# All queries and keys transposed by TensorE instead of the DMA crossbar in a gated linear attention with a feed-forward layer

## The chip, the core and the metric

The kernel runs on one core of a Trainium2 chip. The metric is the device time in microseconds of one execution. It is 247.29 us, the median of three runs of the kernel before (247.19 to 247.33).

## The reference

The inputs are q, k, v and the complex decay a_re + i a_im, each 4 batches x 8 heads x 768 steps x 48 channels in f32, and three weights of a gated layer (384 x 1536, 384 x 1536 and 1536 x 384). The reference is a recurrence over time per batch and head, and then the gated layer over its 3,072 rows:

```
mag = sqrt(a_re^2 + a_im^2);  scale = min(mag, 0.999) / (mag + 1e-6)
for t in range(768):
    S_re, S_im = ar*S_re - ai*S_im + k[t] (x) v[t],  ar*S_im + ai*S_re
    y[t] = q[t] . S_re                       # 48-vector times 48x48 state
x   = y, heads side by side, [3072, 384]
out = (sigmoid(x @ w_gate) * (x @ w_val)) @ w_out
```

## The kernel before

Time is cut into 6 chunks of 128 steps. One batch of one chunk is a slab, so there are 24 slabs m = 0 to 23, each with all 8 heads. Slabs are handled in groups of 2 or 4 (`SIZES`, line 51) in the stage on decays, and in pairs (`PAIR`) in the feed-forward layer.

For each slab the kernel loads a_re, a_im, k, q and v (SP queue, line 552), takes logarithms and angles of the decays, sums them over the chunk with a triangular matmul (steps `cl` and `ct`), and turns the sums into scale and phase (`ee`, `cs`). Step `qke` (line 728) scales q and k, and step `qs` (line 851, always on VectorE) multiplies them by cosine and sine into an f16 tile `slot`, in which each head has 128 columns: time in the 128 partitions.

The scores of a head need k and q with channels in the partitions, so `slot` is transposed: 8 blocks of 128x128 for q and 8 for k per slab. The code has two ways to do it, chosen by `m in CROSSED` (line 866):

- `tp` and `qkT` (lines 888 to 902): for each half of a slab, 8 TensorE transposes against an identity into one PSUM bank (lines 892 and 893), then one copy of 128x1024 f16 from PSUM to the tile `qkT`, on VectorE or ScalarE (`copied`, lines 519 and 521), as `HOME["qkT"]` has it.
- `xk` and `xq` (lines 870 to 876): two DMAs per slab with the crossbar's transpose, issued from the SP queue (line 871), which write the two `qkT` tiles from `slot` with no compute engine and no PSUM bank.

In the kernel before, slabs 0 to 5 go the first way and slabs 6 to 23 the second.

From there both ways are alike: `sc` (line 911, 4 matmuls for each half of a slab) makes the scores, `mst` (line 926, VectorE) masks them out of PSUM, `kv` and `P` (lines 958 and 968) add to the state, `u` and `x16` scale it by the chunk's decay, `y` (lines 984 and 986) makes the output rows, `y16`, `xp`, `xt` bring them to f16 and transpose them for the next layer. For each pair of slabs the layer follows: `pg` and `pv` (line 1043, six matmuls of 256 columns each per step), a tanh (line 1054, ScalarE), the product `p` (line 1061, VectorE), `po` (line 1082, 12 matmuls of 384 columns per slab, in three steps), `ot` (out of PSUM) and `st`, the store.

The order of all instructions is written out ahead: each step has a due time in `TIMES`, the steps are emitted sorted by it (`Plan.order`, line 341), and every engine and the SP queue work through their own share of that order without overtaking. The due times are used here only as an order. `SLOTS` says which buffer each tile takes, in the same order. `HOME` says for each step that can run on several engines which one takes it (v VectorE, a ScalarE, g GpSimd). `WARM` (line 303) says ahead of which steps dummy matmuls of 128 columns on zeros are run (line 1131), 131 in all.

Of the kernel before, what the change touches and what calls it, by code (L numbers as in the profile page):

```python
# [27 lines left out]
CROSSED = range(6, 24)  # L28
# [6 lines left out]
    "sq": "vagvaaggaagagagaaggagggg",  # L35
    "add": "vvvvgggggggggggggggggggg",
    "lh": "gvggggvggggg",
    "r": "vvgggggggggg",
    "v16": "vavagaggggagggggagavaaga",
    "qke": "vvvggggvggggggggggggvggg",  # L40
    "th": "aagvaagvgaav",
    "ab": "vvavvavaavaaaaaaaaaavaaa",
    "qkT": "vavavvvvavvvvvvvvvvvvvvvvvvvvvvvvvvvvvvvvvvvvvvv",
    "P": "vava",
    "u": "ggggggvggggggggggvgg",
    "x16": "ggaavgaggggvggag",
    "y16": "avvvaavvavavvvavaaavaaaa",
    "xt": "vvvvvvavvvvvavvavvvvvaav",
    "ot": "vvvvvaaavvvvavvaaavvaaavv",
# [4 lines left out]
        27.89, 36.02, 27.27],  # L54
    "wv": [
        31.35, 38.17, 36.03],
    "wo": [
        53.47, 54.3, 65.03],
    "lr": [
        0.75, 2.68, 7.03, 7.06, 24.34, 27.88, 25.83, 26.32, 45.89, 58.15,  # L60
        53.31, 52.18, 71.46, 92.9, 87.25, 85.33, 106.38, 121.07, 118.57,
        112.93, 170.37, 176.96, 133.38, 160.02],
    "la": [
        2.22, 1.85, 10.78, 7.07, 24.5, 26.36, 25.84, 27.87, 48.76, 56.39,
        53.93, 53.32, 75.86, 92.85, 87.77, 85.34, 111.4, 121.08, 121.86,
        118.56, 176.57, 178.21, 153.22, 134.91],
    "sq": [
        7.04, 7.02, 11.86, 9.9, 24.95, 29.54, 26.34, 29.5, 49.21, 58.89,
        56.85, 62.71, 83.72, 96.51, 92.96, 86.01, 112.9, 129.56, 128.24,
        118.61, 180.83, 185.55, 167.29, 170.36],  # L70
    "add": [
        7.05, 7.9, 13.4, 13.88, 26.35, 38.15, 28.5, 38.12, 53.3, 65, 62,
        65.86, 87.2, 96.54, 96.47, 92.92, 121.81, 129.58, 128.25, 129.55,
        184.23, 185.57, 169.56, 170.39],
    "lna": [
        9.92, 14.99, 33.31, 67.86, 98.47, 139.01, 185.56, 171.42],
    "lh": [
        8.54, 14.47, 40.53, 42.65, 69.29, 75.89, 102.61, 103.34, 136.22,
        141.84, 185.59, 172.91],
    "lnm": [  # L80
        11.87, 15.39, 38.16, 66.46, 100.65, 132.15, 185.58, 170.4],
    "inv": [
        9.93, 16.37, 36.01, 70.07, 103.36, 139.02, 186.18, 172.85],
    "r": [
        10.77, 19.16, 40.52, 39.65, 73.59, 75.88, 108.19, 107.9, 142.65,
        142.64, 189.11, 173.82],
    "cl": [
        14.97, 14.96, 17.84, 16.27, 45.44, 42.85, 47.17, 46.54, 70.89, 76.95,
        80.11, 77.54, 104.14, 104.52, 114.2, 116.75, 138.97, 140.17, 148.32,
        149.93, 187.16, 186.78, 181.01, 173.23],  # L90
    "ee": [
        16.91, 14.98, 18.49, 17.83, 47.18, 44.65, 48.42, 47.56, 72.96, 79.27,
        86.25, 79.29, 106.53, 106.39, 114.78, 117.62, 140.01, 141.81, 149.19,
        152.85, 189.76, 189.77, 182.5, 173.81],
    "scr": [
        35.3, 38.13, 41.19, 37.26, 52.64, 53.49, 54.34, 53.48, 87.94, 92.86,
        95.76, 92.91, 118.58, 111.43, 121.83, 124.54, 153.21, 155.22, 160.22,
        160.21, 195.89, 195.1, 187.57, 187.58],
    "rbt": [
        46.92, 48.74, 55.48, 96.46, 126.03, 161.47, 198.36, 188.29],  # L100
    "arr": [
        50.09, 50.04, 55.92, 98.24, 127.86, 161.92, 205.03, 188.88],
    "lk": [
        16.93, 15.41, 15.42, 17.85, 30.76, 49.23, 53.94, 66.48, 75.91, 85.35,
        94.86, 88.08, 112.25, 92.84, 112.27, 118.55, 125.19, 156.21, 161.95,
        146.39, 185.54, 190.51, 161.93, 181.02],
    "lq": [
        16.94, 16.28, 16.95, 21.91, 41.18, 50.73, 62.72, 69.68, 79.24, 92.87,
        95.78, 88.09, 112.26, 104.92, 122.21, 118.59, 155.19, 156.9, 161.96,
        146.4, 190.31, 197.73, 161.94, 190.12],  # L110
    "lv": [
        15.4, 29.55, 9.91, 26.79, 30.86, 50.74, 71.28, 66.47, 52.19, 92.94,
        76.96, 95.79, 133.17, 121.82, 125.2, 146.64, 160.01, 154.52, 171.41,
        166.24, 140.93, 180.62, 192.37, 195.11],
    "v16": [
        15.89, 30.3, 14.95, 27.29, 45.52, 60.69, 71.29, 84.58, 87.19, 101.96,
        114.07, 118.91, 136.26, 130.58, 142.92, 147.37, 164.44, 155.21,
        178.63, 169.53, 167.28, 202.72, 198.62, 205.05],
    "qke": [
        17.82, 16.36, 20.04, 24.35, 48.73, 53.28, 67.87, 71.45, 84.59, 93.48,  # L120
        96.49, 92.93, 112.96, 108.55, 134.93, 121.8, 157.53, 160.03, 167.43,
        157.52, 209.72, 205.09, 191.58, 190.32],
    "atan": [
        14.48, 21.92, 40.57, 75.9, 108.2, 143.28, 191.6, 176.95],
    "ct": [
        15.44, 15.43, 22.66, 24.05, 48.2, 49.65, 58.14, 59.2, 83.81, 87.93,
        91.11, 87.21, 116.85, 121.09, 130.19, 122.59, 151.79, 158.27, 164.99,
        155.16, 205.89, 202.2, 191.28, 189.92],
    "r16": [
        15.45, 18.69, 23.57, 25.71, 49.24, 50.7, 58.9, 59.78, 84.57, 89.07,  # L130
        91.94, 87.95, 117.61, 121.2, 132.12, 123.7, 152.84, 159.36, 165.57,
        156.87, 207.37, 204.03, 192.35, 190.49],
    "nid": [
        16.92, 19.28, 24.33, 26.3, 49.49, 52.17, 59.3, 60.37, 85.16, 89.47,
        92.89, 88.87, 118.54, 121.4, 132.33, 124.35, 153.03, 160, 166.46,
        157.5, 208.97, 205.07, 192.97, 191.11],
    "cr": [
        20.92, 23.58, 25.85, 28.76, 50.72, 53.37, 62.74, 64.56, 87.18, 91,
        95.81, 89.85, 119.29, 122.19, 134.27, 126.29, 156.88, 161.48, 167.96,
        157.86],  # L140
    "ab": [
        17.28, 20.91, 26.31, 26.78, 52.62, 53.29, 60.7, 63.2, 87.24, 91.46,
        95.8, 89.46, 118.9, 122.61, 134.26, 126.3, 155.17, 162.17, 167.97,
        158.26, 209.12, 205.47, 195.76, 192.33],
    "cs": [
        21, 23.59, 26.51, 30.73, 52.63, 54.33, 65.04, 65.87, 88.07, 92.06,
        98.25, 91.47, 121.01, 124.52, 134.92, 126.94, 156.89, 162.18, 170.33,
        160.19, 209.71, 205.48, 195.77, 192.34],
    "qs": [
        21.9, 24.04, 29.56, 33.52, 54.31, 56.84, 67.89, 72.97, 89.48, 94.21,  # L150
        98.26, 92.95, 122.6, 125.18, 136.25, 128.26, 157.55, 163.7, 175.58,
        160.2, 210.61, 207.38, 198.38, 192.88],
    "tp": [
        24.94, 24.49, 26.86, 25.82, 30.88, 33.51, 34.4, 34.25, 56.38, 61.19,
        63.19, 59.9],
    "qkT": [
        26.18, 26.33, 27.86, 28.51, 34.86, 34.87, 38.11, 38.14, 59.65, 61.99,
        63.91, 61.2],
    "sc": [
        30.87, 26.8, 29.51, 30.31, 36, 35.29, 39.63, 38.75, 63.38, 62.7,  # L160
        64.55, 65.43, 76.51, 76.73, 80.49, 79.88, 99.76, 98.23, 103.88,
        103.37, 108.76, 108.54, 110.29, 105.52, 133.14, 130.57, 133.37,
        132.11, 144.9, 144.91, 141.57, 146.38, 167.92, 166.23, 170.32, 170.09,
        182.04, 182.27, 179.73, 179.08, 219.4, 218.3, 218.53, 215.46, 205.46,
        204.01, 202.19, 202.47],
    "mst": [
        30.89, 27.26, 31.34, 30.74, 37.25, 35.55, 40.05, 39.66, 64.58, 63.18,
        64.99, 65.85, 79.26, 77.55, 82.04, 82.03, 102, 99.99, 104.53, 103.57,
        110.54, 110.53, 114.09, 106.37, 133.57, 132.13, 134.9, 133.19, 145.74,
        145.73, 144.93, 148.33, 168.49, 167.42, 171.45, 170.52, 184.25,  # L170
        183.56, 182.51, 181.03, 220.93, 221.67, 220.95, 217.02, 205.91,
        204.43, 204.02, 204.04],
    "kv": [
        30.75, 40.06, 77.33, 35.62, 84.19, 72.09, 98.02, 90.24, 111.38,
        111.17, 121.02, 125.17, 144.87, 141.37, 152.83, 166.03, 180.81,
        171.19, 180.6, 186.17],
    "P": [
        39.64, 45.46, 79.28, 40.54, 87.17, 75.87, 101.65, 90.99, 112.95,
        112.94, 121.1, 127.85, 144.94, 142.63, 153.44, 168.15, 183.57, 186.38,
        181.05, 192.36],  # L180
    "y": [
        31.46, 33.3, 37.89, 42.66, 67.91, 67.88, 87.23, 85.97, 102.59, 105.07,
        116.74, 121.03, 136.85, 137.26, 146.6, 148.7, 171.4, 171.84, 186.37,
        183.14, 221.99, 221.25, 207.36, 205.1],
    "y16": [
        34.24, 34.88, 38.76, 42.68, 69.67, 69.27, 88.11, 86.71, 103.55,
        105.77, 116.76, 121.13, 138.98, 139, 148.73, 149.96, 172.01, 172.45,
        187.59, 187.81, 222.6, 222.41, 207.97, 205.88],
    "xp": [
        34.85, 35.83, 41.17, 44.62, 71.27, 70.08, 88.7, 87.76, 104.91, 106.36,  # L190
        121.11, 121.19, 140, 140.55, 149.2, 150.97, 172.9, 173.07, 189.75,
# [970 lines left out]
```

## Time and profile before

| | value |
|---|---|
| median of three runs | 247.29 us |
| profiled execution, its own time | 246.99 us |
| span of that execution, first to last instruction | 244.9 us |
| PE (TensorE) busy | 215.4 us, 88% |
| VectorE (DVE) busy | 206.3 us, 84% |
| ScalarE (ACT) busy | 198.6 us, 81% |
| GpSimd (POOL) busy | 145.9 us, 60% |
| bytes moved by DMA | 41.75 MB, 170 GB/s over the span |
| crossbar DMAs, all on the SP queue | 36, first issued at 72.8 us, last at 218.8 us |
| TensorE's granted clock | 1.000 |

The span is 2.1 us shorter than the execution's own time, since it begins with the first instruction and ends with the last. Busy time of PE includes the pipeline's latency (a matmul of 128 columns is recorded with 219 ns while the next begins 56 ns later), so a busy PE can still have gaps; the starts of the matmuls show these.

### The profile page before, as it was taken

To read this page: it belongs to the slowest core of one execution; us is meant where nothing else is said; L and a number is where in the kernel's file an instruction comes from. 1 tells how busy PE (TensorE), PEld (TensorE's weight loads), DVE (VectorE), ACT (ScalarE), POOL (GpSimd) and SP (SyncE) were. 2 spreads that over 40 slices of the span, in tenths; PEclk is the share of its full clock that TensorE was granted. 3 is DMA by queue.
4 is the path that set the end of the run, shared out by engine and by line. 5 is a ranking of instruction groups with operands and counts; after the bars stand their busy time and mean duration, and the time that the engine had idled before them with its cause. 6 is when DMAs were issued, how large, how long until landed. Compare 5 with 4: busy or idle time off the path is not lost.

```text
span 244.9 us, 6068 instructions
## 1 busy us (share of the span) xinstructions
PE 215.4 (88%) x2319; PEld 168.5 (69%) x2319; DVE 206.3 (84%) x317; ACT 198.6 (81%) x326; POOL 145.9 (60%) x138
## 2 busy tenths in 40 slices
PE   0376899959787997999999999999999999999993
PEld 0234688738556865778867778877788777788981
DVE  4589999999888999999999979989887977988250
ACT  2899899948599989999989999996899995542341
POOL 2305977895567899758659986499776683100000
PEclk9999999999999999999999999999999999999999
DMA  7999999999999999999999998979999569073011
GB/s 144 215 218 212 197 183 192 177 191 175 177 180 137 202 244 186 196 177 219 197 192 205 195 212 172 220 165 178 196 191 205 131 136 197 35 141 98 3 64 66
DMA packets 171004, 41.75 MB, mean 170 GB/s; under 512 B 163916, under 2 KB 170976, under 8 KB 170976
## 3 DMA queue, kind: packets, MB, share of 16 engines
q1 hardware_dynamic: 166800, 37.80, 78.3%
q0 software_dynamic: 4176, 3.57, 9.6%
q8 instruction: 18, 0.29, 0.5%
q14 instruction: 10, 0.08, 0.1%
HBM read 30.67 MB, written 4.72 MB: 145 GB/s over the span
## 4 chain that ended last, share of the span: by engine, by line
PE 50%; DVE 15%; ACT 13%; SPq 8%; DMA 8%; issue 4%; DVEq 0%; ACTq 0%
PE banks L1043 25%; PE banks L1082 15%; SPq L552 7%; DMA qk<-in_q_dram 5%; DVE a L768 3%; DVE slot L851 3%; PE banks L911 2%; DVE p L1061 2%; ACT g L1054 2%; DMA qk<-in_k_dram 2%; PE banks L783 2%; DMA a<-in_a_im_dram 1%; DVE qk L728 1%; DVE r L798 1%; ACT lm L604 1%
## 5 line engine op out<-in xcount | busy, mean ns | idle before, releaser
L1061 DVE SCALAR_TENSOR_TENSOR p<-g,banks 128x512 f16<-128x512 f16 x72 | 47.7, 681 | 12.5 <-ACT g L1054 7.4
L1043 PE MATMUL banks<-xt,wg 128*128 128x256 f16 x432 | 56.0, 273 | 0.7 <-DVE xt L521 0.4
L1043 PE MATMUL banks<-xt,wv 128*128 128x256 f16 x432 | 56.2, 273 | 0.0
L1082 PE MATMUL banks<-wo,p 128*128 128x384 f16 (+1 forms) x300 | 55.5, 320 | 0.5 <-ACT g L1054 0.3
L1054 ACT ACTIVATE g<-banks 128x512 f16<-128x512 f32 x72 | 41.2, 601 | 16.8 <-PE banks L1043 11.6
L1043 PEld LDWEIGHTS <-wg 128*128 128x128 f16 x432 | 40.9, 98 | 7.8 <-issue 1.5
L1043 PEld LDWEIGHTS <-wv 128*128 128x128 f16 x432 | 41.4, 98 | 6.8 <-issue 0.5
L728 POOL TENSOR_TENSOR qk<-qk,ee 128x768 f32<-128x768 f32 x19 | 35.3, 1863 | 14.5 <-ACT cr L815 6.8
L851 DVE TENSOR_TENSOR slot<-qk,banks 128x1536 f16<-128x1536 f32 x24 | 41.8, 1745 | 1.7 <-issue 1.3
L1082 PEld LDWEIGHTS <-p 128*128 128x128 f16 x300 | 27.7, 97 | 14.6 <-issue 1.6
L1125 ACT ACT_TABLE_LOAD x28 | 35.9, 1283 | 0.5
L926 DVE TENSOR_TENSOR mst<-banks,msk_t 128x512 f16<-128x512 f32 x48 | 31.9, 685 | 3.4 <-PE banks L911 2.9
L647 POOL TENSOR_TENSOR a<-a 128x768 f32<-128x768 f32 x10 | 18.7, 1884 | 10.7 <-ACT a L641 8.6
L591 POOL TENSOR_TENSOR lm<-sq 128x384 f32<-128x384 f32 x20 | 21.2, 1064 | 4.2 <-ACT sq L583 3.8
L585 POOL TENSOR_TENSOR sq<-a 128x768 f32<-128x768 f32 x12 | 18.2, 1513 | 6.2 <-DMA a<-in_a_im_dram 4.3
L911 PEld LDWEIGHTS <-qkT 128*128 128x128 f16 x192 | 13.2, 97 | 3.2 <-DVE qkT L521 1.1
L940 POOL TENSOR_TENSOR state<-state,arr 128x384 f32<-128x384 f32 x15 | 12.5, 837 | 4.2 <-DVE arr L697 3.4
L583 ACT ACTIVATE sq<-a 128x768 f32<-128x768 f32 x10 | 8.6, 856 | 7.9 <-DMA a<-in_a_re_dram 7.8
L658 PE MATMUL banks<-lm,wl_t 128*128 128x384 f32 x8 | 4.6, 700 | 10.9 <-ACT lm L604 10.9
L768 DVE SCALAR_TENSOR_TENSOR a<-a 128x768 f16<-128x768 f32 x10 | 13.8, 1409 | 0.0
L798 DVE TENSOR_SCALAR r<-banks 128x384 f16<-128x384 f32 x24 | 13.2, 549 | 0.6 <-PE banks L783 0.4
L815 ACT ACTIVATE cr<-banks 32x384 f32<-32x384 f32 x20 | 9.7, 484 | 4.7 <-PE banks L805 4.0
(93 smaller groups left out, 411.8 us busy)
## 6 DMA issues: line engine op xcount, KB each, us to landing
a<-in_a_re_dram SPq DMA_DIRECT2D x24, 192.0 KB
a<-in_a_im_dram SPq DMA_DIRECT2D x24, 192.0 KB
v<-in_v_dram SPq DMA_DIRECT2D x24, 192.0 KB
qk<-in_k_dram SPq DMA_DIRECT2D x24, 192.0 KB
qk<-in_q_dram SPq DMA_DIRECT2D x24, 192.0 KB
out_dram<-ot SPq DMA_DIRECT2D x23, 192.0 KB
wg<-in_moe_w_gate_dram POOLq DMA_DIRECT2D x3, 384.0 KB, 7.7
wv<-in_moe_w_val_dram POOLq DMA_DIRECT2D x3, 384.0 KB, 10.6
```

The source lines that it names most:

```text
L585: on.tensor_tensor(out=T[SQ], in0=T[A][:, :, s], in1=T[A][:, :, s], op=ALU.mult)
L591: home("add", m).tensor_tensor(out=T[LM][:, s], in0=T[SQ][:, 0], in1=T[SQ][:, 1], op=ALU.add)
L647: home("r", w).tensor_tensor(out=T[A][:, 1, i:j], in0=T[A][:, 1, i:j], in1=T[A][:, 0, i:j], op=ALU.mult)
L728: home("qke", m).tensor_tensor(out=T[QK], in0=T[QK], in1=T[EE], op=ALU.mult)
L768: nc.vector.scalar_tensor_tensor(out=turns(T)[:, i:j, 1], in0=T[A][:, 1, i:j], scalar=1.0 / TWO_PI, op0=ALU.mult, in1=turns(T)[:, i:j, 0], ...
L851: nc.vector.tensor_tensor(out=T[SL].rearrange("p i h (r x) -> p r i h x", r=2)[:, :, :, :, 0:D], in0=T[QK].rearrange("p i (h d) -> p i h d ...
L926: nc.vector.tensor_tensor(out=T[MS][:, :n_], in0=T[SC], in1=msk_t.unsqueeze(1).broadcast_to([L, n_, L]), op=ALU.mult)
L1043: nc.tensor.matmul(T[ACC][:, r], wt[:, j, f0:f0 + 128], T[XT][:, :, j], start=(j == 0), stop=(j == 2))
L1054: nc.scalar.activation(out=T[G16], in_=T[PG], func=FT.Tanh, scale=0.5)
L1061: nc.vector.scalar_tensor_tensor(out=T[PT][:, 2 * fp:2 * fp + 2], in0=T[G16], scalar=1.0, op0=ALU.add, in1=T[PV], op1=ALU.mult)
L1082: nc.tensor.matmul(T[PO][:, :wd], T[PT][:, fb, s0:s0 + L], wo16[:, fb, c0:c0 + wd], start=(fb == 0), stop=(fb == NFB - 1))
L1125: nc.scalar.preload_act_table_set(SETS[key[1]])
```

## The change

The set of slabs that go through the crossbar becomes empty: slabs 6 to 23 are transposed as slabs 0 to 5 were. The 36 steps `xk` and `xq` are gone, 36 steps `tp` (288 TensorE transposes) and 36 steps `qkT` (36 copies out of PSUM) come in. All due times, buffer numbers, engine choices and dummy matmuls are new; the functions of the kernel are as they were. In the diff, each row of `TIMES` and `SLOTS` is replaced; the rows shown are those of the steps that come, go or are referred to.

```
-CROSSED = range(6, 24)
+CROSSED = ()
...
 HOME = {
-    "sq": "vagvaaggaagagagaaggagggg",
+    "sq": "vagvggaagaaagagaggagvggg",
     "add": "vvvvgggggggggggggggggggg",
-    "lh": "gvggggvggggg",
-    "r": "vvgggggggggg",
-    "v16": "vavagaggggagggggagavaaga",
-    "qke": "vvvggggvggggggggggggvggg",
-    "th": "aagvaagvgaav",
-    "ab": "vvavvavaavaaaaaaaaaavaaa",
-    "qkT": "vavavvvvavvvvvvvvvvvvvvvvvvvvvvvvvvvvvvvvvvvvvvv",
-    "P": "vava",
-    "u": "ggggggvggggggggggvgg",
-    "x16": "ggaavgaggggvggag",
-    "y16": "avvvaavvavavvvavaaavaaaa",
-    "xt": "vvvvvvavvvvvavvavvvvvaav",
-    "ot": "vvvvvaaavvvvavvaaavvaaavv",
+    "lh": "vgggggggggvg",
+    "r": "vvggggggvvvg",
+    "v16": "ggggaggaggaaggaggggggaga",
+    "qke": "vvvgvggvgggggggggggggggg",
+    "th": "aavgggagagvg",
+    "ab": "vvvavaavaaaaaaaavaaaaaaa",
+    "qkT": "vvvvvvvvvvvvvvaavvavvvavavvvvvavaaavvvvavaavavva",
+    "P": "vaaa",
+    "u": "ggggggggggggggggvggg",
+    "x16": "gggggaggggaggagv",
+    "y16": "aaavavaaavvaaaavvaavaava",
+    "xt": "vvvvvavvvavvvvavvvvvvaav",
+    "ot": "vvvavavavaavvvvaaaavvavvv",
 }
...
     "tp": [
-        24.94, 24.49, 26.86, 25.82, 30.88, 33.51, 34.4, 34.25, 56.38, 61.19,
-        63.19, 59.9],
+        21.72, 26.53, 26.54, 24.19, 35.45, 34.69, 32.72, 31.38, 60.78, 58.8,
+        60.33, 63.19, 69.1, 64.68, 75.72, 76.17, 92.98, 93.43, 93.88, 98.44,
+        104.97, 105.83, 106.27, 100.4, 125.58, 126.68, 134.63, 128.16, 145.52,
+        144.9, 135.08, 137.45, 168.34, 167.24, 170.05, 174.68, 182.14, 181.14,
+        176.64, 177.73, 220.12, 220.57, 222.63, 223.43, 206.66, 205.57,
+        208.47, 207.36],
...
     "pg": [
-        37.24, 38.1, 43.23, 42.69, 42.7, 36.58, 45.88, 53.92, 55.73, 52.61,
-        49.22, 53.27, 72.29, 79.23, 80.71, 72.95, 74.1, 78.57, 91.95, 89.59,
...
+        38.3, 36.48, 41.11, 37.14, 42.53, 43.58, 51.62, 58.87, 47.73, 47.27,
+        58.82, 54.97, 72.03, 87.31, 79.63, 73.34, 74.86, 72.69, 86.5, 86.49,
...
-    "xk": [
-        75.93, 79.44, 96.52, 102.6, 108.18, 99.11, 126.31, 126.39, 141.85,
-        140.02, 164.45, 167.94, 178.22, 175.93, 215.7, 213.52, 203.36, 202.18],
-    "xq": [
-        75.92, 79.43, 96.53, 102.62, 107.24, 105.51, 126.04, 127.84, 144.86,
-        140.57, 164.49, 167.95, 180.61, 165, 217.04, 214.81, 203.37, 202.14],
 }
...
 WARM = {
-    ('cl', 3): 5,
-    ('ct', 2): 43,
-    ('sc', 0, 1): 3,
-    ('sc', 1, 0): 3,
-    ('sc', 1, 1): 3,
-    ('sc', 0, 0): 11,
-    ('y', 1): 29,
-    ('kv', 3): 4,
-    ('kv', 1): 3,
-    ('pv', 0, 0): 5,
-    ('pv', 1, 4): 3,
-    ('pg', 1, 3): 5,
-    ('ct', 7): 3,
-    ('y', 5): 1,
+    ('cl', 0): 22,
+    ('ct', 1): 5,
+    ('ct', 3): 57,
+    ('sc', 0, 0): 1,
+    ('sc', 1, 1): 4,
+    ('sc', 0, 1): 7,
+    ('y', 1): 34,
+    ('kv', 1): 10,
+    ('kv', 0): 7,
+    ('sc', 3, 1): 4,
+    ('pg', 0, 0): 1,
+    ('pg', 1, 5): 9,
+    ('ct', 7): 10,
+    ('pv', 2, 5): 5,
     ('cl', 8): 5,
-    ('pv', 2, 5): 5,
 }
```

## The prediction

> **What bounds the kernel now.** I read the page's busy times and slices first, to see which engine is full and where.
>
> ```profile
> PE 215.4 (88%) x2319; PEld 168.5 (69%) x2319; DVE 206.3 (84%) x317; ACT 198.6 (81%) x326; POOL 145.9 (60%) x138
> ...
> PE   0376899959787997999999999999999999999993
> ...
> DMA  7999999999999999999999998979999569073011
> ```
>
> Three engines are above 80%, and DMA is at nine tenths for three quarters of the span. PE is full only from the second third on. So the second view is busy time by stretches, cut where the order of steps can be cut too: at 77.6 us the first `pg` of the pair of slabs 4 and 5 starts, at 148.4 us that of slabs 12 and 13.
>
> ```profile
> 0.00:50.00 50.00, 33.38 (x378) 25.87 (x379) 42.50 (x68) 43.17 (x66) 28.26 (x33) 1.00 1.05 193
> 50.00:77.60 27.60, 21.54 (x230) 15.98 (x230) 23.83 (x35) 20.63 (x34) 18.54 (x18) 1.00 1.07 173
> 77.60:148.40 70.80, 67.97 (x741) 52.52 (x740) 66.90 (x103) 67.88 (x109) 57.79 (x51) 1.00 1.04 199
> 148.40:241.00 92.60, 92.54 (x974) 74.17 (x972) 73.03 (x114) 66.44 (x120) 41.31 (x39) 1.00 0.65 139
> ```
>
> After the two times the columns are PE, PEld, DVE, ACT, POOL, granted clock, DMA share, GB/s. From 148.4 us on PE is busy 92.54 of 92.6 us; between 77.6 and 148.4 us all three engines are above 94%. Busy PE can hide gaps, so I took the starts of all matmuls from the timeline and counted as standstill what lies between two starts beyond the pitch of their kind (56 ns for 128 columns, 109 for 256, 162 for 384, 25 for 48): 19.1 us before 77.6, 6.1 us from there to 148.4, 1.0 us after.
>
> Third, the chain in order of time, in the middle and at the end:
>
> ```profile
> 80.42 1.33 SPq L871
> 82.41 3.52 DMA a<-in_a_im_dram
> ...
> 115.54 4.25 DMA qk<-in_k_dram
> ```
>
> ```profile
> 229.18 7.86 PE banks L1043 x72
> 237.04 3.91 PE banks L1082 x24
> 240.97 0.49 ACT ot L512
> ```
>
> Until about 127 us the chain passes through ScalarE, VectorE, the SP queue and loads; from there to 241 us nearly every long piece is PE. In the first part the crossbar does cost: its packets and the loads share engines and the SP queue, which does this in one stretch:
>
> ```profile
> 95.67 0.44 SPq L552 DMA_DIRECT2D qk<-in_q_dram  x1
> 96.16 0.57 SPq L552 DMA_DIRECT2D v<-in_v_dram  x1
> 96.83 8.32 SPq L871 DMA_TRANSPOSE qkT<-slot  x5
> ```
>
> **The change part by part.** What each operation costs is in the rows of slabs 0 to 5, which go TensorE's way already:
>
> ```profile
> L892 PE MATMUL banks<-idn_t,slot 128*128 128x128 f16 x48 | 6.3, 219 | 1.3 <-ACT qkT L519 0.9 <-DVE p L1061 0.3 <-ACT banks L827 0.2
> ...
> L521 DVE COPY qkT<-banks 128x1024 f16<-128x1024 f16 x9 | 6.0, 682 | 0.9 <-PE banks L893 0.9
> ...
> L519 ACT ACTIVATE qkT<-banks 128x1024 f16<-128x1024 f16 x3 | 3.1, 1017 | 0.0
> ```
>
> *Removed:* 36 crossbar DMAs. Their 36,864 packets of 256 bytes (9.44 MB) take 54.6 us of all 16 DMA engines together, and their issues 36 x 1.285 = 46.3 us of the SP queue, plus some 30 us in which that queue waited for `slot` with loads and stores behind it. None was issued before 72.8 us, so the 19.1 us of early standstill owe them nothing. Later they can only hurt PE through its 6.1 + 1.0 us.
>
> *Added on PE:* 18 slabs x 16 = 288 transposes. The record is 219 ns, but starts are 56 ns apart (median of L892 and L893): 16.1 us, all on the engine that sets the end.
>
> [...] Here the row decides: 56 ns, and the granted clock is 1.00 in both stretches that hold the 96 transposes of before.
>
> *Added elsewhere:* by the `HOME` strings the copies out of PSUM go from 9 to 34 on VectorE and from 3 to 14 on ScalarE. With the other engine choices (r +3 and sq +1 on VectorE; v16 -3, y16 -3, th, ab, P, u, x16 -1 each) VectorE gets 25 x 0.68 + 3.8 - 5.7 = +15.2 us; ScalarE 11 x 1.02 - 1.7 = +9.5; GpSimd +2.5, of 99 us idle. ScalarE's table loads stay at 28 in the new order.
>
> *Order:* I used both `TIMES` tables as orders only, priced each step by its row, and summed what stands ahead of the first `pg` of slabs 4 and 5, then of slabs 12 and 13, then the rest.
>
> - Ahead of slabs 4 and 5: PE 41.0 to 42.2 us (2 of the new `tp` stand here, 0.9 us), VectorE 66.2 to 68.2, ScalarE 70.9 to 72.6. Taken as **0**: PE's 19.1 us of standstill, VectorE's 11.3 us and ScalarE's 13.8 us of idle time cover it. Without cover on PE it is 1.2. The 50 added dummies, 2.8 us, stand nearly all here, under the same standstill.
> - To slabs 12 and 13: PE 64.6 to 70.8 (18 `tp`, 8.1 us, and 1.9 us of other work moved out), VectorE +2.8 against 3.9 us idle, ScalarE +1.0 against 2.9. The least is 0.1, if the shorter queue of loads lets PE use all of its 6.1 us; the most is 6.2, if none. I take **+2.8**, what VectorE gets, since PE waits for tiles that VectorE makes.
> - The rest: PE 91.9 to 100.6, 16 `tp` of it. **+8.7**, since PE stands still 1.0 us in 92.6. VectorE's +10.3 and ScalarE's +7.6 fit into 19.6 and 26.2 us idle. Least 7.7.
> - The end (24 matmuls of `po`, `ot`, a store, some 8 us from 237) has the same steps in the new order: 0.
>
> *New wait:* the matmuls `sc` now wait for a copy that stands in VectorE's queue behind `qs`, `p` and `mst`, and every PE instruction behind `sc` waits too. In slabs 0 to 5 PE's idle time on this was
>
> ```profile
>   DVE qkT L521: 1.6, 5
> ...
>   ACT qkT L519: 0.3, 1
> ```
>
> 1.9 us for 12 halves; 36 halves at that rate give 5.7 us. The bounds are 0 (other matmuls stand between `tp` and `sc`) and 5.7. I take 0, because the feed-forward steps fill this place from 77 us on: `sc` waited 0 there for crossbar tiles, with a far longer way.
>
> *Sum* against the profiled execution, 246.99 us (its span of 244.9 and 2.1 around it): 246.99 + 0 + 2.8 + 8.7 = 258.5. The median of the runs is 0.3 above that execution, so **258.8**.
>
> [...]
>
> **The rivals.**
>
> 1. *Loads come earlier and PE uses all of its standstill after 77.6 us.* 246.99 + 0.3 + 0.1 + 7.7 = 255.1. For it: SP and DMA pieces on the chain around 80 and 112 us. Against: VectorE and ScalarE are 95% busy there and get more work.
> 2. *The copies come late,* VectorE paces the middle, and PE waits at `sc` throughout: 258.8 + 5.7 = 264.5; with the middle's 6.2 for 2.8 it would be 267.9. For it: VectorE at 66.9 of 70.8 us. Against: 20% idle later.
> 3. *Faster: the opening shrinks.* The order of the first 77.6 us is new, and PE stands still for 19.1 us of it. It decides once more than 11.5 us of that (258.8 - 247.3) is gone; with all of it gone the time is 239.7. Against: the opening runs on loads, 15 issues in a row and a q tile landing at 17.4 us, and the PE work ahead of the cut is the same apart from transposes.
>
> That the change does nothing is ruled out by the 288 added instructions.
>
> **How the numbers follow.** My forecast has 0.50, rival 1 0.20, rival 2 0.23, rival 3 0.05, and 0.02 is left for a partial rival 3 that ends near no change. A measurement of this kernel tells 0.2%, about 0.5 us. So slower has 0.93, same 0.02, faster 0.05. The range reaches from rival 1 less half a microsecond, 254.5, to rival 2 and one more, 265.5: it leaves out rival 3 and the worse half of rival 2.
>
> **What would show it.** In the profile after: no crossbar on the SP queue; 384 transposes at 56 ns; PE with about 16 us more work, and a last stretch, from the first `pg` of slabs 12 and 13, longer by about 9 us with under 2 us standstill; that step itself 2 to 4 us later; 34 copies `qkT` on VectorE at 0.68 us; loads landing sooner after their issue. I would be wrong if PE shows idle time on `qkT` above 3 us, if transposes start more than 60 ns apart, or if the cut at slabs 4 and 5 moves by more than 2 us.

## The result, and the profile after

The changed kernel takes 259.75 us (median of four runs, 259.54 to 262.81) against 247.31 us for the kernel before: 1.0516 times as long, 95% interval 1.0443 to 1.059. The forecast was 258.8. Ratios here and below leave out executions over 1.5% above the fastest of their kernel, which are 267.13 and 267.99 us of the four with the copies doubled in slabs 6 to 11, and 297.27 and 297.46 us of the four with the crossbar again; the profiles of these two kernels are of their longest execution.

The page of the changed kernel, busy time and slices:

```profile
PE 239.2 (92%) x2657; PEld 191.8 (73%) x2657; DVE 217.4 (83%) x335; ACT 209.2 (80%) x336; POOL 147.1 (56%) x146
...
PE   3497999888939999999999999999999999999994
...
PEclk9999999997995999999999999999999999999999
DMA  7999999989987754986133077552671122410011
```

PE is up by 23.8 us of busy time, DMA is no longer full after the first third, and TensorE's granted clock has dents in slices 10 and 13 that the profiled execution of the kernel before did not have. The windows of the changed kernel, cut at the same steps as before (`pg` of slabs 4 and 5, now at 80.3 us; `pg` of slabs 12 and 13, now at 155.0; the end of the last matmul), columns as in the prediction:

```profile
0.00:80.30 80.30, 62.95 (x682) 49.06 (x683) 65.26 (x103) 67.35 (x101) 49.04 (x55) 0.96 1.04 189
80.30:155.00 74.70, 74.50 (x861) 60.15 (x860) 68.97 (x105) 69.49 (x116) 57.32 (x55) 0.98 0.56 119
155.00:257.10 102.10, 101.64 (x1121) 82.58 (x1118) 83.09 (x129) 71.89 (x120) 40.75 (x37) 1.00 0.34 78
```

This profiled execution took 262.81 us, 3 us more than the other three. A second profile of the same kernel, taken for the experiments, fell on an execution of 259.80 us, nearer to the median:

```profile
0.00:77.50 77.50, 61.03 (x681) 47.60 (x682) 64.37 (x103) 65.93 (x99) 48.89 (x54) 0.98 1.03 187
77.50:152.10 74.60, 73.27 (x863) 59.24 (x860) 72.58 (x105) 70.41 (x118) 59.41 (x56) 1.00 0.60 129
152.10:254.20 102.10, 101.62 (x1121) 82.60 (x1118) 83.04 (x129) 71.86 (x120) 41.07 (x37) 1.00 0.33 78
```

The two agree in the middle and the last stretch to 0.1 us and differ by 2.8 us in the opening. With the stretches of before (77.4, 70.8 and 92.6 us when cut at the same events), and PE's work and standstill counted from the starts of the matmuls as in the prediction:

| stretch | before: length, work, standstill | after, first profile | after, second profile | change in length |
|---|---|---|---|---|
| to `pg` of slabs 4 and 5 | 77.4, 49.1, 18.3 | 80.3, 52.8, 26.4 | 77.5, 52.8, 23.6 | +2.9 / +0.1 |
| to `pg` of slabs 12 and 13 | 70.8, 64.9, 5.9 | 74.7, 71.4, 3.3 | 74.6, 71.4, 3.2 | +3.9 / +3.8 |
| to the last matmul | 92.6, 91.8, 0.6 | 102.1, 100.5, 1.4 | 102.1, 100.5, 1.5 | +9.5 / +9.5 |

(Work and standstill fall a little short of the length where matmuls follow each other a few per cent above their pitch, or run at half clock. The counts of before differ by up to 0.8 us from those in the prediction, since f32 matmuls and the edges are taken slightly differently here.) The rows of the new operations:

```profile
L894 PE MATMUL banks<-idn_t,slot 128*128 128x128 f16 x192 | 25.9, 220 | 0.4 <-ACT y L514 0.2
L895 PE MATMUL banks<-idn_t,slot 128*128 128x128 f16 x192 | 25.8, 220 | 0.0
L523 DVE COPY qkT<-banks 128x1024 f16<-128x1024 f16 x34 | 22.9, 684 | 3.2 <-PE banks L895 3.0
L913 PE MATMUL banks<-qkT 128*128 128x128 f16 x192 | 17.6, 223 | 0.3 <-DVE qkT L523 0.3
L521 ACT ACTIVATE qkT<-banks 128x1024 f16<-128x1024 f16 x14 | 14.2, 1021 | 3.1 <-PE banks L895 3.1
```

The scores (L913) waited 0.3 us in all for copies. At the end the chain is PE, piece after piece:

```profile
249.40 3.93 PE banks L1045 x36
253.33 3.91 PE banks L1084 x24
```

### The profile page after: what moved, and what is told of

Its sections match the earlier page's. It is cut to its first block, busy times and chain, and to the rows that moved or that the text cites. A ratio compares the mean times of both kernels' runs of the same rounds, so it can differ in the third digit from the quotient of the medians.

```text
span 261.0 us, 6729 instructions
## 1 busy us (share of the span) xinstructions
PE 239.2 (92%) x2657; PEld 191.8 (73%) x2657; DVE 217.4 (83%) x335; ACT 209.2 (80%) x336; POOL 147.1 (56%) x146
## 4 chain that ended last, share of the span: by engine, by line
PE 69%; ACT 15%; DMA 7%; DVE 3%; SPq 3%; issue 2%; ACTq 0%
PE banks L1045 30%; PE banks L1084 16%; DMA a<-in_a_im_dram 4%; ACT L1127 3%; PE banks L913 3%; PE banks L894 3%; PE banks L895 3%; DMA a<-in_a_re_dram 3%; PE banks L785 2%; PE banks L664 2%; SPq L554 2%; ACT g L1056 2%; PE banks L988 2%; PE banks L1020 2%; ACT sq L585 2%
## 5 line engine op out<-in xcount | busy, mean ns | idle before, releaser
L1045 PE MATMUL banks<-xt,wg 128*128 128x256 f16 x432 | 58.7, 280 | 0.1
L1063 DVE SCALAR_TENSOR_TENSOR p<-g,banks 128x512 f16<-128x512 f16 x72 | 47.8, 680 | 7.2 <-ACT g L1056 3.6
L1045 PEld LDWEIGHTS <-wg 128*128 128x128 f16 x432 | 42.1, 100 | 8.3 <-issue 1.1
L730 POOL TENSOR_TENSOR qk<-qk,ee 128x768 f32<-128x768 f32 x19 | 36.9, 1948 | 20.1 <-DMA qk<-in_q_dram 10.3
L894 PE MATMUL banks<-idn_t,slot 128*128 128x128 f16 x192 | 25.9, 220 | 0.4 <-ACT y L514 0.2
L895 PE MATMUL banks<-idn_t,slot 128*128 128x128 f16 x192 | 25.8, 220 | 0.0
L523 DVE COPY qkT<-banks 128x1024 f16<-128x1024 f16 x34 | 22.9, 684 | 3.2 <-PE banks L895 3.0
L593 POOL TENSOR_TENSOR lm<-sq 128x384 f32<-128x384 f32 x20 | 20.1, 1032 | 8.2 <-ACT sq L585 7.8
L894 PEld LDWEIGHTS <-slot 128*128 128x128 f16 x192 | 18.7, 98 | 2.1 <-DVE slot L853 1.1
L895 PEld LDWEIGHTS <-slot 128*128 128x128 f16 x192 | 18.9, 98 | 1.5 <-issue 0.9
L913 PE MATMUL banks<-qkT 128*128 128x128 f16 x192 | 17.6, 223 | 0.3 <-DVE qkT L523 0.3
L942 POOL TENSOR_TENSOR state<-state,arr 128x384 f32<-128x384 f32 x16 | 15.0, 940 | 4.4 <-DVE arr L699 4.2
L521 ACT ACTIVATE qkT<-banks 128x1024 f16<-128x1024 f16 x14 | 14.2, 1021 | 3.1 <-PE banks L895 3.1
```

The source lines that it names most:

```text
L523: on.tensor_copy(out=dst, in_=src)
L730: home("qke", m).tensor_tensor(out=T[QK], in0=T[QK], in1=T[EE], op=ALU.mult)
L894: nc.tensor.transpose(tp[:, 4 + i], T[SL][:, 1, h], idn_t)
L895: nc.tensor.transpose(tp[:, i], T[SL][:, 0, h], idn_t)
L913: nc.tensor.matmul(sc[:, 4 * hf * both + i], kt, qt, start=True, stop=True)
L1045: nc.tensor.matmul(T[ACC][:, r], wt[:, j, f0:f0 + 128], T[XT][:, :, j], start=(j == 0), stop=(j == 2))
```

## The experiments

Two theories were set against each other. *PE's issue time:* the loss is 56 ns for each added transpose, in full where PE is full. *The copies:* the loss is the way from transpose over copy to scores, and the load on VectorE and ScalarE. Beside them stood two questions of size: what the freed SP queue and DMA are worth, and what the opening does. Where a kernel below has an order of its own, buffers were given anew to fit it. The kernel before was run beside each group of kernels, with medians of 246.35, 246.85 and 247.17 us, so a difference of times between groups is uncertain by half a microsecond and more.

### Twice the transposes, twice the copies, in slabs 12 to 23

```
-for i in range(4):                       # step tp
+for i in [*range(4)] * (1 + (12 <= m < 24)):
```

> In slabs 12 to 23 every transpose is issued twice into the same place (192 more, 56 ns each); copies and order as in the changed kernel. If PE's issue time is what counts, the time rises by 10.8 us to 270.5 (269 to 271.5). If what counts is the copies out of PSUM or the wait from transpose to copy to scores, it rises by 0 to 3 us, since the copies are the same.

```
-copied(home("qkT", n), T[QT], T[TP])     # step qkT
+for _ in range(1 + (24 <= n < 48)):
+    copied(home("qkT", n), T[QT], T[TP])
```

> In slabs 12 to 23 every copy qkT out of PSUM is made twice (14 more on VectorE, 9.5 us; 10 more on ScalarE, 10.2 us); the transposes are as in the changed kernel. If PE's issue time is what counts, the time rises by 0 to 1.5 us, since VectorE and ScalarE are idle 20% and more in this part. If the copies pace it (the second rival), it rises by 5 us or more, to 265 or above.

Measured: 270.60 us with the transposes doubled (ratio to before 1.1007, 1.0924 to 1.109) and 271.25 with the copies doubled (1.1051, 1.0971 to 1.1131). The first theory met the first number (270.5) and was wrong by 10 us on the second (at most 261.3); the second theory was wrong by 8 us on the first (at most 262.8) and right on the second (265 or above). That the first number is met to 0.1 us is partly luck: by ratio the kernel is 12.3 us above the changed kernel, and of the profiles' difference of 11.6 us, 1.8 lie in the opening, where nothing was added, and 2.5 in the middle, for 3.6 us of transposes. The last stretch of each shows more. Transposes doubled, then copies doubled:

```profile
156.40:265.80 109.40, 108.76 (x1249) 89.69 (x1246) 84.81 (x128) 71.37 (x120) 42.11 (x37) 1.00 0.29 68
```

```profile
152.70:264.70 112.00, 104.49 (x1122) 82.60 (x1119) 93.04 (x139) 79.71 (x128) 42.02 (x37) 1.00 0.30 71
```

With the transposes doubled, PE is busy all the time and its standstill is 1.6 us: the stretch grows by 7.3 us, for 128 more transposes (7.2 us; the other 64 lie in the stretch ahead). With the copies doubled, PE's work is the same 100.5 us, but its standstill goes from 1.4 to 11.3 us. In the changed kernel VectorE and ScalarE were idle 19.0 and 30.2 us of 102.1 there, more than the 10.0 and 7.8 us by which their busy time grew, and still they could not take the second copies in for nothing. So in the kernel as it is, PE's issue time sets the pace of this stretch (1.4 us standstill), but the copies are only just in time. That idle time of an engine was no slack. Whether the second copies cost so much by the longer way to the scores or by the place that they take in the two queues was not separated.

### Half of the transposes' PE work left out, slabs 12 to 23

```
+for i in range(4) if m >= 12 else ():
+    nc.tensor.matmul(two blocks of tp as f32, T[SL][:, i % 2, hf * 4 + i], zero, ...)
-for i in range(4):
+for i in range(4) if m < 12 else ():
```

> The changed kernel, with half the PE work of the transposes left out in slabs 12 to 23: per half 4 matmuls against zeros, each over the width of two blocks, in place of 8 transposes, so these slabs are computed with zeros; copies, waits and order are as they were. 96 matmuls of 56 ns fewer are 5.4 us: 254.2 us (253 to 255.5) if PE's issue time is what counts there. If the copies hold the pace, as doubling them suggested, the time stays above 257.

Measured: 257.72 us (255.91 to 259.53; ratio 1.0432, 1.0357 to 1.0507), 1.8 us below 259.55, the median of the changed kernel run again, where the first theory had 5.4 us less. By time alone that is nearer to the copies. But the four executions are two pairs: 255.9 and 256.2 us at a mean granted clock of 0.993 and more, 259.3 and 259.5 at 0.980. The changed kernel's one execution at 0.980 took 262.8 us and its executions at 0.99 and more 258.0 to 260.3, so like against like the gain is about 3.5 us. By stretch, the profiled execution (259.53 us, of the longer pair) has the last stretch at 98.8 us against 102.1, 3.3 us for 64 matmuls (3.6 us) left out; the middle at 73.9 against 74.6; and an opening of 81.2 against 77.5, which has the same instructions in both. The opening's own spread, below, hides half of the gain in the median. PE's issue time counts in the last stretch when it is halved as when it is doubled; in the middle 32 matmuls fewer (1.8 us) brought 0.7 us.

### The same two in the middle, slabs 6 to 11

> The changed kernel with the transposes of slabs 6 to 11 issued twice (96 more, 5.4 us). PE stands still 3.2 us between the two marked steps: between 2.2 and 5.4 us slower, 261.8 to 265, if PE's issue time counts there as well; within 1 us of 259.55 if VectorE alone paces the middle.

> The changed kernel with the copies of slabs 6 to 11 made twice (8 on VectorE, 5.5 us, 4 on ScalarE, 4.1 us). If VectorE paces the middle, as the prediction had it for this stretch, 4 to 7 us slower (263.5 to 266.5); if PE alone does, 0 to 1.5 us.

The edits are those above with other slabs. Transposes doubled: 261.69 us (1.0611, 1.0548 to 1.0673), 2.1 us slower. The middle takes 77.2 us for 74.6. Of the 96 added transposes 80 (4.5 us) stand there: PE's work is 75.9 for 71.4 and its standstill 1.3 for 3.2, so 1.9 us of the 4.5 went into gaps. Copies doubled: 1.0682 times before (1.0619 to 1.0745), 264.0 us at 247.17 for before, 4.5 us slower than the changed kernel. In its profile PE's work in the middle is unchanged at 71.4, and its standstill rises from 3.2 to 8.8 us, of which some 1.6 are half clock (the mean granted clock of this execution is 0.987). So both count in the middle: 9.6 us of copies, 5.5 of them on VectorE, cost 4.5, and 5.4 us of transposes cost 2.1, which per microsecond added is about the same. The prediction took it that VectorE paces this stretch. These runs do not show that. With the transposes doubled PE stood still 1.3 us there, and VectorE was idle for 6.2 us:

```profile
77.55:154.75 77.20, 77.04 (x941) 63.72 (x939) 71.05 (x105) 70.70 (x118) 58.35 (x55) 1.00 0.58 123
```

And in the two profiles of the changed kernel, above, VectorE's busy time in the middle is 68.97 and 72.58 us for the same 105 operations, 5.7 and 2.0 us idle, while the stretch takes 74.7 and 74.6 us.

### The same transposes without an order made for them

In the order of the kernel before, only `xk` and `xq` were taken out and `tp` and `qkT` put in ahead of the scores that need them:

```
-CROSSED = range(6, 24)
+CROSSED = ()                 # before_late_tp: (6, 7, 8, 9, 10, 11,)
 TIMES: xk, xq out; tp about 2.6 ahead of sc (less or more where banks are short), qkT 0.1 behind tp
```

> The kernel before with its own order, engine choices and dummies, but all slabs transposed by TensorE: each new tp is put some 2.6 us (1 to 8 where PSUM banks are short) ahead of its scores, its copy right behind; the 36 new copies are all on VectorE, as HOME of before has them. Buffers are given anew. If PE's issue time is what the change costs, 16.1 us are added of which up to 5 fall into the middle's standstill: 246.4 + 11 to 16 = 257.5 to 262.5 us, and the new order is worth little. If the copies pace it, 24.5 us on VectorE alone give 265 us or more, and the new order's shift of copies to ScalarE has bought the difference.

> As before_all_tp, for slabs 12 to 23 alone (192 transposes, 24 copies on VectorE); slabs 6 to 11 stay on the crossbar. If PE's issue time counts fully where PE is full: 246.4 + 10.8 = 257.2 (256 to 258.5). If the copies pace it: 260 or above. If the late part had room: below 252.

Measured: 293.19 us for all slabs (1.1889, 1.1837 to 1.1941) and 274.01 for slabs 12 to 23 (1.1101, 1.1051 to 1.115). That is 46 and 27 us above before, two and a half to three times what PE's issue time accounts for (16.1 and 10.8). The waits of the first, from 77 us on, VectorE then PE:

```profile
DVE qkT L421 <- PE banks L793: 27.7, 24, 2.9
```

```profile
PE banks L943 <- DVE qkT L421: 5.6, 8, 0.9
PE banks L562 <- DVE mst L826: 3.5, 1, 3.5
PE banks L811 <- DVE qkT L421: 3.1, 5, 0.8
PE banks L982 <- DVE qkT L421: 2.8, 2, 2.1
```

(The columns are us in total, times, longest.) VectorE comes to the copy and waits for the transposes, 27.7 us in 24 places, with all its other work behind it; PE comes to the scores and waits for the copy, and later feed-forward matmuls wait as well. PE stands still 23.3 us in the middle and 13.2 in the last stretch. The new order, in which the copies are shared with ScalarE (34 and 14) and stand behind other work, brings 293 down to 260. How much of this is the place of the copies, how much the share of ScalarE, and how much the rest of the new order was not separated. The prediction took that order as given and did not see how much hangs on it.

### The crossbar again in the new order, slabs 12 to 23

```
-CROSSED = ()
+CROSSED = range(12, 24)
 TIMES: tp, qkT of these slabs out; xk, xq 1.9 behind the start of qs
```

> Half of the change undone: in the changed kernel's own order, slabs 12 to 23 go through the crossbar again (24 DMAs, each issued about when its slot tile is ready); slabs 6 to 11 stay on TensorE. If the loss is PE's issue time where PE is full, 24 halves x 8 transposes x 56 ns = 10.8 us come back: 259.75 - 10.8 = about 249 us, with PE's last stretch shorter by 9 to 11 us. If the loss was made by the new order and the opening, the time stays within 1.5 us of 259.75.

Measured: 1.1947 times before (1.183 to 1.2063), about 294 us (292.58 to 297.46), worse than either kernel, and neither theory expected it. The SP queue gives the likely reason:

```profile
114.88 0.70 SPq L447 DMA_DIRECT2D a<-in_a_re_dram  x1
131.32 2.73 SPq L766 DMA_TRANSPOSE qkT<-slot  x2
```

```profile
SPq L766 <- DVE slot L746: 36.5, 6, 15.7
```

The queue waits for `slot` 36.5 us in six places, once for 15.7 us, and nothing behind it is issued. The loads that should have gone out in that time are late:

```profile
POOL qk L623 <- DMA qk<-in_q_dram: 44.6, 5, 17.1
```

A wait at the crossbar DMAs alone does not do this: in the kernel before that queue waited there for some 30 us too, in pieces of at most 6.6 us. So this is no clean way back: a crossbar DMA in a queue that also carries the loads needs its place as much as a copy on VectorE does. As a test of the loss it failed.

### Traffic of the crossbar put back

```
+spare = [const.tile([L, 8, L], F16, name=f"spare{i}") for i in range(3)]
 ...
+nc.sync.dma_start_transpose(out=spare[n % 3], in_=wg16[:, 0, :1024])   # at each of the 36 new tp
```

> The changed kernel with 36 crossbar transposes of 256 KB put back as traffic only: issued on the SP queue at the places of the 36 new tp, from a weight tile that is long loaded, into spare tiles that nobody reads. It shows what the freed SP queue and DMA engines are worth. If PE sets the end, loads later by some us cost 0 to 3 us (259.5 to 262.5). If the relief is large (first rival), 4 us or more.

Measured: 271.71 us (1.1014, 1.0974 to 1.1054), 12.2 us above 259.55; of the two cases of the expectation, the relief of 4 us or more is met and the 0 to 3 us that PE as the bound would give are wrong. SP waits hardly at all for this (3.1 us for a spare tile), but the middle and the last stretch become

```profile
79.70:160.60 80.90, 75.33 (x862) 60.73 (x860) 69.64 (x105) 69.88 (x116) 57.77 (x55) 0.95 0.89 173
160.60:266.10 105.50, 102.48 (x1121) 82.67 (x1118) 83.53 (x129) 72.17 (x120) 40.78 (x37) 1.00 0.60 122
```

6.3 and 3.4 us longer, at the same PE work, with 9.5 and 4.8 us of standstill. DMA's share in the middle is 0.89 for 0.60, and GpSimd's wait for q in the whole remainder is 20.0 us for 10.2. The largest single wait of PE is not for a load, though. It is for ScalarE, which waits with `ot` for a buffer that a store has to empty first:

```profile
114.57 4.79 SPq L799 DMA_TRANSPOSE spare<-wg  x3
121.66 1.26 SPq L1013 DMA_DIRECT2D out_dram<-ot  x2
124.69 0.49 ACT L414 ACTIVATE ot<-banks 128x384 f32<-128x384 f32 x1 [6.73 <-issue]
```

```profile
PE banks L867 <- ACT ot L414: 5.4, 1, 5.4
```

The first of these two stores had its data at 105.5 us, was issued at 121.66, behind loads and crossbar DMAs in the SP queue, and landed at 124.6; `ot` starts then. The granted clock is half from 122.0 to 128.8 us, behind this wait. So much of the loss in the middle is one store kept back in the SP queue, of which the 36 added issues take 60.8 us; how much of the rest is the transfers themselves was not separated. In the kernel before, PE's standstill in the middle was 5.9 us with its own 36 crossbar DMAs, in an order made with them. What the crossbar had taken is worth 10 to 12 us in this order, and the changed kernel has used it up: with such DMAs at these places the change would have cost about 24 us in place of 12.

### The opening

> The changed kernel itself once more, as the base for the others on this chip. 258.5 to 260.5 us. If the opening varies with the landing of one load, its step pg of slabs 4 and 5 starts anywhere from 76 to 80.3 us, later by as much as ScalarE waits for a_im ahead of its square of slab 10 (0 to 5 us).

```
 TIMES (changed kernel)
-"lr" 9, 10: 58.89, 58.9;  "la" 10: 60.34;  "lv" 5, 7: 47.25, 58.88
+"lr" 9, 10: 53.0, 53.1;   "la" 10: 53.2;   "lv" 5, 7: 60.35, 61.0
```

> Changed kernel, three loads of decays (a_re of slabs 9 and 10, a_im of slab 10) moved ahead of a_re of slab 11 in the SP queue, two loads of v (slabs 5 and 7) moved behind them; all else alike. In the changed kernel ScalarE waits 4.9 us for a_im before its square of slab 10, and TensorE's clock is halved for 6.8 us after the standstill that follows. If the opening's loss is this load's place in the order, the step pg of slabs 4 and 5 starts 2 to 5 us earlier, the clock stays at 1.0 there, and the time is 255 to 258 us. If the opening's loss is the PE work or the backlog of all loads, it stays within 1 us of 259.75.

The changed kernel again: 259.55 us (257.96 to 260.34). With the earlier loads 258.76 (256.46 to 260.15); by ratios to before 1.0555 (1.0474 to 1.0636) against 1.0508 (1.0471 to 1.0546), so no difference is shown. In the profile of the edited kernel ScalarE's wait is gone and `pg` of slabs 4 and 5 starts at 74.3 us, but one execution proves little here. Up to this step, six of the kernels have the same instructions in the same order:

| profile | ScalarE's wait for the load ahead of its square of slab 10 | `pg` of slabs 4 and 5 starts at |
|---|---|---|
| late_copy_twice | none | 76.0 |
| after_again | none | 77.5 |
| late_xbar | none | 77.7 |
| late_tp_twice | 3.8 us | 79.3 |
| after | 4.9 us | 80.3 |
| late_tp_half | 5.3 us | 81.2 |

In the first profile of the changed kernel that wait is this row, 4.89 us behind a load that took 10.28 us to land (window of the opening, ScalarE, and the chain):

```profile
67.67 0.84 ACT L585 ACTIVATE sq<-a 128x768 f32<-128x768 f32 x1 [4.89 <-DMA a<-in_a_im_dram]
```

```profile
57.28 10.28 DMA a<-in_a_im_dram
67.67 0.84 ACT sq L585
```

One load that lands early or late from execution to execution goes with 76.0 to 77.7 us or 79.3 to 81.2 us. That it is the cause was not separated from the backlog of all loads.

Last, two small moves in the kernel before, meant to shorten its opening:

```
-HOME["qke"] = "vvvggggvgg..."    "qke" 4, 5: 48.73, 53.28   "lr" 9: 58.15   "lv" 8: 52.19
+HOME["qke"] = "vvvgvvgvgg..."    "qke" 4, 5: 50.72, 53.0    "lr" 9: 52.2    "lv" 8: 66.5
```

> The kernel before with two small moves in its opening: qke of slabs 4 and 5 goes from GpSimd to VectorE, behind the two steps tl that in before take 2.55 us each while GpSimd works on qke (0.95 us each later in the run, with GpSimd elsewhere); a_re of slab 9, for which ScalarE waits 3.2 us, is loaded earlier, and v of slab 8 later. If the opening moves all that follows, 1.5 to 3.5 us are gained: 243 to 245 us. If PE makes up such delays later, the time stays within 0.5 us of before.

Measured: 248.39 us (1.0069, 1.0041 to 1.0097), 0.7% longer and not shorter. The two `tl` steps took 0.94 us each where they had taken 2.55, as meant, but the chain then went over the small copy of row sums:

```profile
54.11 7.15 DMA rows_t<-ee
61.35 0.43 PE banks L579 x4
```

That transfer of 1.5 KB landed 7 us after its issue, and PE waited 5.4 us for it. In the kernel before PE's longest wait for such a copy between 30 and 80 us was 1.4 us. That the load moved forward made it late is likely, but was not separated from the other moves. No version faster than before was found.

## Why the prediction was right, and where not

- **The sum.** 0 + 2.8 + 8.7 = 11.5 us was forecast, 12.4 measured. In the second profile the stretches give 0.1 + 3.8 + 9.5 - 0.2 (the end) = 13.2 us of span.
- **Transposes at 56 ns, 16.1 us on PE.** Right: PE's work rises from 205.8 to 224.7 us over the three stretches, 18.9 us, which is 16.1 and 2.8 for the dummies. The record of one transpose, 220 ns here, is not the price of transposes in a row: the next one begins 56 ns later, within the record of the one ahead.
- **The rest, +8.7.** Measured +9.5: 8.7 more work, 7.2 of it the 128 new transposes that stand there, and 0.9 more standstill. Doubling and halving moved this stretch by 7.3 and -3.3 us for 7.2 and -3.6 us of work.
- **The middle, +2.8.** Measured +3.8; both bounds (0.1 and 6.2) held. The reason given, that VectorE's added work paces it, is not shown: PE got 6.5 us of work and lost 2.7 us of standstill, VectorE's busy time grew by 2.1 us in one profile and 5.7 in the other at the same length, and doubled copies and doubled transposes cost about the same per microsecond added. That the term came within 1 us is in part luck; which chain sets this stretch stays open.
- **The opening, 0.** Right for the second profile (+0.1). In the first it moved by 2.9 us, beyond the 2 us that I had named as a sign of error. There the step failed that took standstill for cover: the longer opening goes with a late load and with 6.8 us more of half clock (the last section), and which of them made it longer was not shown.
- **The new wait, 0.** The size was right (0.3 us at the scores, where 5.7 was the other bound). The reason was wrong. I said that VectorE and ScalarE have idle time for the copies; twice the copies cost 11.5 us all the same, and the same transposes in the old order 46 us. The new order, with its shares and buffers, keeps this wait at nothing.
- **The relief, at most 7.1 us.** The bound was drawn from PE's standstill in the old order. It does bound what the old order could gain. It does not bound what the new order spends: the same traffic put back costs 12.2 us there. That the middle came out at +3.8 and not at +6.5, its added work, fits this relief, but no run separates it.

Rival 1 (all standstill used) did not happen: 3.2 of 5.9 us remained in the middle. Rival 2 is a state that the kernel is close to, not the one it is in. Rival 3 found nothing in the opening.

## What to carry to other kernels

Where PE was full to the end, work moved onto it cost its issue time, start to start (9.5 us of length for 8.7 us of work in the last stretch), and that was forecast to a microsecond from rows of the same operation elsewhere in the trace. Whether the rest of the chain stays hidden depended on the order in the queues: the same 288 transposes cost 12 us in an order made for them and 46 us in one that was not, and a crossbar DMA that waited for its tile held back the loads behind it in its queue (for 36.5 us in all). Double a cost that you believe to be hidden before you call it free; here idle time on its engine did not show it: VectorE and ScalarE were idle 19.0 and 30.2 us in the last stretch, and twice the copies still made it 9.9 us longer.

## What was not expected of the hardware

TensorE's clock. In the changed kernel the granted clock is halved for 3.4 us from 60.0 us and for 6.8 us from 77.0 us in the first profile, and for 3.4 us from 46.1 us in the second (0.98 over its first 77.5 us); in the profiled execution of the kernel before it is not, from 13.8 us to the end. Other executions of that kernel show a lower clock: beside the changed kernel's second run, six of 16 had a mean granted clock of 1.000 and ten of 0.986 to 0.993. In the 3.4 us up to the start of a dent in the first profile PE was busy 1.75 us (from 56.6 us) and 0.69 us (from 73.6 us). In the kernel before a stretch of the same length with 1.76 us (51.3 to 54.7 us) was followed by a clock of 1.00, so PE's busy time ahead does not tell the two apart, and what brings a dent about was not shown. At half clock the transposes start 107 ns apart and are recorded with 314. By these starts, 107 ns for 56, a period of 3.4 us costs at most 1.6 us, an estimate, and less where PE waits anyway; the first profile, with 6.8 us more of it and the later load, took 3 us longer than the second.

Most of the transposes ran at the full clock: 272 of the changed kernel's 384 start after 83.9 us of the first profile, and from there to the end the granted clock is 1.00. In `before_all_tp`, where all slabs go TensorE's way too, it is 1.00 from 160 to 290 us. What a transpose itself does to the clock was not separated.

And VectorE beside GpSimd: the step `tl` on VectorE takes 0.95 us alone (at 155.8 and 156.6 us of the kernel before) and took 2.55 us twice, at 47.8 and 50.3 us there, while GpSimd worked on `qke` and, in the end, on the step behind it. Work on GpSimd does not always do this: at 167.1 us of the changed kernel, beside a `qke` from 167.3 us on, the step took 0.95 us.
